# Two batches through both MLPs together, instead of batch 0 ahead: an attention and MoE kernel on one core

## The chip, the cores and the metric

The kernel runs on one core of one Trainium2 chip. The metric is the device time of one execution in microseconds. Three runs of the kernel before took 1252.75, 1256.22 and 1260.56 us; the median, 1256.22, is what a changed kernel is held against.

## The reference

Four batches of twelve heads, 448 tokens, head size 64, all inputs float32 (the weights arrive as float64 and are rounded). Attention's output, tokens by 768 features, goes through two bias-free MLPs in a row:

```python
q_n, k_n = rmsnorm(q, g_q), rmsnorm(k, g_k)
attn = softmax(q_n @ k_n.T / 8)                 # per head, with max subtracted and 1e-9 in the sum
x = (attn @ v), heads side by side              # (4 * 448, 768)
h = x @ w_in;  x = maximum(0.01 * h, h) @ w_out # 768 -> 2048 -> 768
a = x @ w1;  b = x @ w2                         # 768 -> 1024 each
out = ((a * b) @ w3) @ w_last                   # 1024 -> 1024 -> 768
```

## The kernel before

**Precision.** Every large product is made of three matmuls in float32r: a value is split into a high part (ScalarE copy) and a low part (subtraction on VectorE or GpSimd), and high x high, low x high, high x low are summed in PSUM (`group`, L519). Weights come as 64-bit words: `Weights.load` fetches a tile (a DMA to `w64`, two buffers), `to_float32` rebuilds float32 out of the words on GpSimd, ScalarE and VectorE, `split` makes `wh` and `wl`. `product` (L569) takes one weight tile and runs it over the batches that it is given; each batch's sum has a PSUM buffer of its own out of three.

**Attention** is a generator, `attention_steps`, of 50 slots of ten steps, one slot a head. A head is eight score matmuls (`ps`, L285 and L286), four readings of them on VectorE, four exponentials on ScalarE, sixteen transposes (`pt`), four copies of these; a pair of heads shares one group of sixteen value matmuls (`po`). The keys of a pair are prepared ahead: `kt` and `rk` are loaded into single buffers, scaled, split, and four DMAs spread the halves into `ks`, which has two buffers. The sum of the exponentials goes out to DRAM (`rd`) and comes back broadcast over partitions (`rb`). All DMAs are issued by SyncE, one after the other, and a DMA that has to wait holds back those behind it.

**Fillers.** `fill` walks through the attention's steps and puts in as many pieces of another generator as its planned nanoseconds allow. Before: slots 5 to 17 get `combine_weights` (w3 times w_last, tile `pw`); slots 17 to 25 get the first MLP's groups 0 and 1 for batch 0 alone (`early`); from slot 25 on come the same two groups for batch 1 (`late`), and then for both batches the first MLP's groups 2 and 3 and the second MLP's two groups. Since groups 0 and 1 are visited twice, their split parts are written to DRAM on the first visit (`kept_first_mlp_h`, `kept_first_mlp_l`, L488) and fetched back on the second (L472). The rounded float32 weights (`kept_first_mlp`, L477, and `kept_second_mlp`) are written in any case: after attention the last two batches run both MLPs from them, in seven products instead of eight (`last_pair`).

A scheduler with a simulated clock then fixes the order of each engine's instructions from this code order, priorities and dependences, so slots and the place of a filler need not agree.

Of the kernel before, what the change touches and what calls it, by code (L numbers as in the profile page):

```python
# [8 lines left out]
F32 = mybir.dt.float32  # L9
F32R = mybir.dt.float32r  # L10
# [7 lines left out]
B, H, S, D = 4, 12, 448, 64  # L18
NT = B * S
DM, FF, F2 = 768, 2048, 1024  # L20
P = 128
# [6 lines left out]
WT = DM  # L28
PB = 2
# [8 lines left out]
GROUPS = {0: 2, 2: 2, 4: 4, **{i: 8 for i in range(8, 48, 8)}}  # L38
MAX_GROUP = 8
TOGETHER = 2000  # L40
COMBINE_SLOTS = 5, 17
EARLY = 2
PRIORITY = dict(
    values=200, p_transpose=600, scores=600, prep=600, load=100, statistics=100, keys=50
)
# [3 lines left out]
def attention_then_moe(  # L49
# [22 lines left out]
    nc = tc.nc  # L72
# [324 lines left out]
    class Weights:  # L397
# [15 lines left out]

        def size(self, t):
            src, wide = self.sources[t][:2]
            if isinstance(src, tuple):
                return src[0].shape[1]
            return src.shape[1] // (2 if wide else 1)

        def load(self, t):  # L420
            src, wide = self.sources[t][:2]
            n = self.size(t)
            if isinstance(src, tuple):
                return
            if not wide:
                self.raw[t] = wp.tile([P, WT], F32, tag="raw", name="raw")
                nc.sync.dma_start(self.raw[t][:, :n], src)
                return
            x = self.words[t] = cv.tile([P, WT, 2], U32, tag="w64", name="w64")
            with tc.issue_after(start["ins"].ins) if t < 2 else ExitStack():  # L430
                nc.sync.dma_start(x[:, :n], src.rearrange("p (n t) -> p n t", t=2))
# [31 lines left out]
        def split(self, t):  # L463
            src, wide, keep, parts = self.sources[t]
            n = self.size(t)
            if isinstance(src, tuple):
                self.parts[t] = tuple(
                    wp.tile([P, WT // P, P], F32R, tag=tag, name=tag) for tag in ("wh", "wl")
                )
                for y, part in zip(self.parts[t], src):  # L470
                    y = y.rearrange("p k c -> p (k c)")[:, :n].bitcast(F32)
                    nc.sync.dma_start(y, part)  # L472
                self.ready = t + 1
                return
            x = self.raw.pop(t)[:, :n]
            if keep is not None:
                nc.sync.dma_start(keep[0], x)  # L477
            if parts is None:
                parts = tuple(
                    wp.tile([P, WT // P, P], F32R, tag=tag, name=tag) for tag in ("wh", "wl")  # L480
                )
                flat = [y.rearrange("p k c -> p (k c)")[:, :n] for y in parts]
            else:
                flat = parts
            nc.scalar.activation(flat[0], x, AF.Copy)  # L485
            subtract("V", flat[1], x, flat[0])
            for y, part in zip(flat, keep[1:] if keep else ()):
                nc.sync.dma_start(part, y.bitcast(F32))  # L488
            self.parts[t] = parts
            self.ready = t + 1  # L490

# [168 lines left out]

            yield from each(product(ws, bs, gs), result)

    kept, again = {}, {}

    def sources(plan):

        for f, bs, g in plan:
            if f is first_mlp:
                tiles = [w_in[g * KG + m] for m in range(KG)] + [w_out[g, m] for m in range(NO)]
            else:  # L670
                tiles = [w12[g * KH2 + m // 2, m % 2] for m in range(2 * KH2)]
            if (f, g) in kept:
                yield from ((k, False, None, None) for k in again[f, g])
            else:
                twice = sum(x[0] is f and x[2] == g for x in plan) > 1
                names = ("", "_h", "_l") if twice else ("",)
                ks = [
                    [
                        dram.tile([P, w.shape[1] // 2], F32, name=f"kept_{f.__name__}{g}_{i}{e}")
                        for e in names  # L680
                    ]
                    for i, w in enumerate(tiles)
                ]
                kept[f, g] = [k[0] for k in ks]
                again[f, g] = [tuple(k[1:]) for k in ks]
                yield from ((w, True, k, None) for w, k in zip(tiles, ks))
            if f is second_mlp:
                for m in range(NO):
                    w = wc[m, :, g * KH2 : (g + 1) * KH2].rearrange("p k c -> p (k c)")
                    yield w, False, None, None  # L690
# [292 lines left out]
    def plan_ns(plan):  # L983
        n = {first_mlp: KG * KD + NO * KG, second_mlp: 2 * KH2 * KD + NO * KH2}
        return sum(3 * S * NS * len(bs) * n[f] for f, bs, _ in plan)
# [25 lines left out]
    def fill(gen, total, span, until, begin=0):  # L1011

        spent, n = 0.0, 0
        done = False
        while True:
            at = next(steps, None)
            n += 1
            while not done and spent < total * (n - begin) / span:
                c = next(gen, None)
                if c is None:  # L1020
                    done = True
                else:
                    spent += c
            if at is None or at == until:
                break
        for _ in gen:
            pass

    parts_of = [(first_mlp, g) for g in range(NG)] + [(second_mlp, g) for g in range(2)]
    early = [(f, (0,), g) for f, g in parts_of[:EARLY]]  # L1030
    late = [(f, (1,), g) for f, g in parts_of[:EARLY]]
    late += [(f, (0, 1), g) for f, g in parts_of[EARLY:]]

    def run(pool, ws, plan):
        for f, bs, g in plan:
            yield from f(pool, ws, bs, g)

    with tc.tile_pool(name="comb", bufs=1) as pool:
        hi = pool.tile([P, K2, DM], F32R, name="lasth")
        lo = pool.tile([P, K2, DM], F32R, name="lastl")  # L1040
        ws = Weights(
            [
                w
                for k in range(K2)
                for h in range(2)
                for w in [
                    (w_last[j], True, None, (hi[:, j], lo[:, j]))
                    for j in range(h * KH2, (h + 1) * KH2)
                    if k == 0
                ]  # L1050
                + [(w3t[k, h], True, None, None)]
            ]
            + list(sources(early + late))
        )
        blocks = Blocks(list(last_sources()))
        n = slots[1] - slots[0]
        fill(combine_weights(ws, hi, lo), comb_ns, n * per_slot, slots[1], slots[0] * per_slot)
    pool = first_pair.enter_context(tc.tile_pool(name="mlp", bufs=1))
    n = PB * H + 1
    fill(run(pool, ws, early), plan_ns(early), (n - slots[1]) * per_slot, n)  # L1060
    fill(run(pool, ws, late), plan_ns(late), (B - PB) * H * per_slot, None)
    first_pair.close()
    last["pool"] = ctx.enter_context(tc.tile_pool(name="mlp2", bufs=1, reuse_waits="tile"))
    for _ in last_pair():
# [45 lines left out]
```

## Time and profile before

| | |
|---|---|
| median of three runs | 1256.22 us (1252.75 to 1260.56) |
| profiled execution | 1252.88 us, its span 1251.1 us |
| TensorE matmuls | 1151.0 us busy, 5816 |
| VectorE | 769.4 us busy |
| ScalarE | 661.4 us busy |
| GpSimd | 226.5 us busy |
| DMA | 191.44 MB, queue of SyncE 51.0% of 16 engines |
| mean granted clock of TensorE | 0.962 |

Matmuls overlap in their pipeline and their ends are modelled, so TensorE's busy time contains more than the time between two starts. The granted clock is 1.0 at 2.4 GHz and 0.5 at 1.2 GHz.

### The profile page before, as it was taken

To read this page: it belongs to the slowest core of one execution; us is meant where nothing else is said; L and a number is where in the kernel's file an instruction comes from. 1 tells how busy PE (TensorE), PEld (TensorE's weight loads), DVE (VectorE), ACT (ScalarE), POOL (GpSimd) and SP (SyncE) were. 2 spreads that over 40 slices of the span, in tenths; PEclk is the share of its full clock that TensorE was granted. 3 is DMA by queue.
4 is the path that set the end of the run, shared out by engine and by line. 5 is a ranking of instruction groups with operands and counts; after the bars stand their busy time and mean duration, and the time that the engine had idled before them with its cause. 6 is when DMAs were issued, how large, how long until landed. Compare 5 with 4: busy or idle time off the path is not lost.

```text
span 1251.1 us, 16792 instructions
## 1 busy us (share of the span) xinstructions
PE 1151.0 (92%) x5816; PEld 976.7 (78%) x5816; DVE 769.4 (61%) x1449; ACT 661.4 (53%) x1308; POOL 226.5 (18%) x211
## 2 busy tenths in 40 slices
PE   3659898999888999898999999999999999899998
PEld 1438686876566888686888888899999999799997
DVE  6788776779755466663785355267346465954553
ACT  5766766677656556454765465245442434533431
POOL 4232222334212123213542211100000000000000
PEclk9769999888998999998999999999999999899999
DMA  7777768989889975564464243153212121212212
GB/s 226 195 203 214 215 189 269 292 284 290 251 245 273 240 202 162 151 187 137 148 218 130 79 133 134 53 167 110 81 34 76 35 76 42 73 38 73 63 35 97
DMA packets 105221, 191.44 MB, mean 153 GB/s; under 512 B 22992, under 2 KB 61872, under 8 KB 105136
## 3 DMA queue, kind: packets, MB, share of 16 engines
q1 hardware_dynamic: 105136, 190.37, 51.0%
q8 instruction: 45, 0.74, 0.3%
q14 instruction: 40, 0.33, 0.1%
HBM read 136.74 MB, written 43.03 MB: 144 GB/s over the span
## 4 chain that ended last, share of the span: by engine, by line
PE 54%; DMA 14%; DVE 7%; ACT 4%; issue 3%; SPq 2%; POOL 1%; ACTq 0%; DVEq 0%; POOLq 0%
PE ps_mm L527 19%; PE ps_o L527 13%; PE ps_b L527 9%; PE ps_c L527 5%; DMA w<-w_in 3%; DMA w<-w_out 3%; PE ps_a L527 2%; PE pt L327 2%; PE po L121 2%; DMA ks<-kt_sb 2%; DMA kt_sb<-kt 1%; DMA wh<-kept_first_mlp_h 1%; PE ps L285 1%; DVE raw L460 1%; PE ps L286 1%
## 5 line engine op out<-in xcount | busy, mean ns | idle before, releaser
L213 DVE TENSOR_TENSOR wl<-raw,wh 128x512 fp32r<-128x512 f32 (+1 forms) x136 | 112.6, 831 | 73.0 <-ACT wh L485 37.8
L527 PE MATMUL ps_mm<-xh,wh 128*128 128x448 f32 x384 | 146.6, 383 | 10.6 <-DMA wh<-kept_first_mlp_h 6.9
L327 PE MATMUL pt<-ident,p 112*112 112x112 f32 x768 | 115.3, 276 | 42.2 <-ACT pth L101 21.3
L327 PEld LDWEIGHTS pt<-ident,p 112*112 112x112 f32 x768 | 88.1, 141 | 77.2 <-ACT pth L101 27.6
L289 DVE TENSOR_SCALAR_CACHE_REDUCE p<-ps,rs 112x448 f32<-112x448 f32 x192 | 126.1, 676 | 33.8 <-PE ps L286 20.4
L527 PE MATMUL ps_mm<-xh,wl 128*128 128x448 f32 x384 | 145.5, 379 | 1.5 <-DMA wl<-kept_first_mlp_l 1.5
L298 ACT ACTIVATE p<-p,low 112x448 f32<-112x448 f32 x192 | 127.2, 663 | 36.1 <-DVE p L289 35.7
L527 PE MATMUL ps_mm<-xl,wh 128*128 128x448 f32 x384 | 145.1, 378 | 0.0
L451 ACT ACTIVATE w<-w 128x768 uint32<-128x768 uint32 (+1 forms) x80 | 63.7, 797 | 109.3 <-DMA w<-w_in 36.2
L456 DVE SCALAR_TENSOR_TENSOR raw<-w,raw 128x768 uint32<-128x768 uint32 (+1 forms) x80 | 71.4, 892 | 79.9 <-ACT w L454 79.6
L449 POOL TENSOR_SCALAR raw<-w 128x768 f32<-128x768 f32 (+1 forms) x80 | 70.0, 875 | 265.8 <-DVE wl L213 99.5
L527 PE MATMUL ps_mm<-gh,wh 128*128 128x448 f32 x288 | 106.7, 372 | 2.7 <-DMA wh<-kept_first_mlp_h 1.3
L527 PE MATMUL ps_mm<-gh,wl 128*128 128x448 f32 x288 | 105.7, 369 | 0.0
L527 PE MATMUL ps_mm<-gl,wh 128*128 128x448 f32 x288 | 105.4, 367 | 0.0
L527 PE MATMUL ps_o<-gl,wh 128*128 128x448 f32 x288 | 104.7, 365 | 0.0
L527 PE MATMUL ps_o<-gh,wl 128*128 128x448 f32 x288 | 102.5, 365 | 0.0
L527 PE MATMUL ps_o<-gh,wh 128*128 128x448 f32 x288 | 99.4, 366 | 0.8 <-DVE s L940 0.8
L285 PE MATMUL ps<-ks,qh 128*112 128x448 f32 x192 | 80.2, 422 | 16.4 <-DMA ks<-kt_sb 6.7
L527 PEld LDWEIGHTS ps_mm<-xh,wh 128*128 128x128 f32 x384 | 75.1, 196 | 19.9 <-DMA wh<-kept_first_mlp_h 7.4
L213 POOL TENSOR_TENSOR gl<-y,gh 128x448 fp32r<-128x448 f32 x48 | 58.9, 1229 | 161.6 <-ACT gh L101 154.9
L527 PEld LDWEIGHTS ps_mm<-xh,wl 128*128 128x128 f32 x384 | 75.0, 195 | 10.5 <-issue 2.1
L213 POOL TENSOR_TENSOR ql<-qt_sb,qh 128x448 fp32r<-128x448 f32 x48 | 61.1, 1273 | 114.2 <-ACT qh L101 71.0
(129 smaller groups left out, 2556.1 us busy)
## 6 DMA issues: line engine op xcount, KB each, us to landing
w<-w_in SPq DMA_DIRECT2D x16, 768.0 KB, 7.4
w<-w_out SPq DMA_DIRECT2D x24, 512.0 KB, 5.2
w<-w SPq DMA_DIRECT2D x16, 768.0 KB, 4.9
qk_sb<-qk SPq DMA_DIRECT2D x48, 224.0 KB, 4.9
qt_sb<-qt SPq DMA_DIRECT2D x96, 112.0 KB, 4.0
w<-w3t SPq DMA_DIRECT2D x16, 512.0 KB, 4.6
w<-w_last SPq DMA_DIRECT2D x8, 768.0 KB, 6.2
kept_first_mlp<-raw SPq DMA_DIRECT2D x16, 384.0 KB, 4.0
```

Of the source, the lines that this page charges most:

```text
L121: one = nc.tensor.matmul(out, a, x, start=begin, stop=end)
L213: e.tensor_tensor(out, x, y.bitcast(F32), op=ALU.subtract)
L285: nc.tensor.matmul(ps, h["qh"][:, q], h["ks"], start=True, stop=False)
L286: nc.tensor.matmul(ps, h["ql"][:, q], h["ks"], start=False, stop=True)
L289: nc.vector.tensor_scalar(p, ps, h["scale"][:, c : c + 1], None, op0=ALU.mult, op1=ALU.min, accum_out=low,)
L298: exps[i] = nc.scalar.activation(p, p, AF.Exp, bias=low, scale=-1.0, accum_out=h["sum"][:, c : c + 1])
L327: nc.tensor.transpose(pt[:, c * CP : (c + 1) * CP], h["p"][c][:, kc * CP : (kc + 1) * CP], ident[:CP, :CP],)
L449: nc.gpsimd.tensor_scalar(out, h, 0.0, 1.0, op0=ALU.mult, op1=ALU.mult)
L451: nc.scalar.activation(low, low, AF.Copy, scale=2.0**-29)
L456: nc.vector.scalar_tensor_tensor(top, high, 3, top, op0=ALU.logical_shift_left, op1=ALU.bitwise_or)
L460: nc.vector.tensor_tensor(top, top, low, op=ALU.add)
L527: nc.tensor.matmul(ps[:, :n], a, x, start=begin, stop=end, skip_group_check=on)
```

## The change

Batches 0 and 1 go through all six groups together, from slot 25 on. There are no groups for batch 0 alone, hence no second visit and no parts of weights in DRAM: `Weights` loses the branches that wrote and fetched them. `combine_weights` is spread over slots 5 to 25. The number of matmuls on TensorE stays the same, 5620 rows of matmuls and transposes in the program; SyncE's program goes from 721 rows to 647 (a row can hold two like DMAs).

```diff
-COMBINE_SLOTS = 5, 17
-EARLY = 2
+COMBINE_SLOTS = 5, 25
...
         def split(self, t):
             src, wide, keep, parts = self.sources[t]
             n = self.size(t)
-            if isinstance(src, tuple):
-                self.parts[t] = tuple(
-                    wp.tile([P, WT // P, P], F32R, tag=tag, name=tag) for tag in ("wh", "wl")
-                )
-                for y, part in zip(self.parts[t], src):
-                    y = y.rearrange("p k c -> p (k c)")[:, :n].bitcast(F32)
-                    nc.sync.dma_start(y, part)
-                self.ready = t + 1
-                return
             x = self.raw.pop(t)[:, :n]
             if keep is not None:
-                nc.sync.dma_start(keep[0], x)
+                nc.sync.dma_start(keep, x)
...
             subtract("V", flat[1], x, flat[0])
-            for y, part in zip(flat, keep[1:] if keep else ()):
-                nc.sync.dma_start(part, y.bitcast(F32))
...
-    early = [(f, (0,), g) for f, g in parts_of[:EARLY]]
-    late = [(f, (1,), g) for f, g in parts_of[:EARLY]]
-    late += [(f, (0, 1), g) for f, g in parts_of[EARLY:]]
+    plan = [(f, (0, 1), g) for f, g in parts_of]
...
-    n = PB * H + 1
-    fill(run(pool, ws, early), plan_ns(early), (n - slots[1]) * per_slot, n)
-    fill(run(pool, ws, late), plan_ns(late), (B - PB) * H * per_slot, None)
+    fill(run(pool, ws, plan), plan_ns(plan), (B - PB) * H * per_slot, None)
```

The order of TensorE's instructions, before, in head 16 (of 0 to 47; `ps_mm` is a product of the first MLP, `gh` and `gl` the parts of batch 0's hidden layer):

```order
L527 MATMUL ps_mm_2980<-gl_2831,wh_2919 128x448
L527 MATMUL ps_mm_2980<-gh_2830,wl_2920 128x448
L527 MATMUL ps_mm_3029<-gh_2660,wh_2997 128x448
L527 MATMUL ps_mm_3029<-gl_2661,wh_2997 128x448
L527 MATMUL ps_mm_3029<-gh_2660,wl_2998 128x448
L527 MATMUL ps_mm_3029<-gh_2754,wh_2997 128x448
L527 MATMUL ps_mm_3029<-gl_2755,wh_2997 128x448
L327 MATMUL pt_2382<-ident_90,p_2287 112x112
L327 MATMUL pt_2382<-ident_90,p_2298 112x112
L327 MATMUL pt_2382<-ident_90,p_2317 112x112
L285 MATMUL ps_2457<-ks_1742,qh_2186 112x448
L286 MATMUL ps_2457<-ks_1742,ql_2188 112x448
```

And of the changed kernel, in head 18 (`xh_1897` and `xl_1898` are batch 1's features of the pair of heads just finished; the two `ps_mm` are sums of batch 1 that stay open until its last pair):

```order
L511 MATMUL ps_mm_3394<-xl_1898,wh_3224 128x448
L511 MATMUL ps_mm_3394<-xh_1897,wl_3225 128x448
L326 MATMUL pt_2293<-ident_90,p_2215 112x112
L326 MATMUL pt_2293<-ident_90,p_2222 112x112
L326 MATMUL pt_2293<-ident_90,p_2233 112x112
L284 MATMUL ps_2353<-ks_1761,qh_2140 112x448
L285 MATMUL ps_2353<-ks_1761,ql_2142 112x448
L326 MATMUL pt_2303<-ident_90,p_2215 112x112
L326 MATMUL pt_2303<-ident_90,p_2222 112x112
L326 MATMUL pt_2303<-ident_90,p_2233 112x112
```

Between the first score matmul of head 14 and that of head 26 there are 336 `ps_mm` matmuls before and 55 now; 13 more now stand in head 13. The 384 `pw` matmuls end in head 13 in both.

SyncE's order before, where the same stretch prepares a pair of heads:

```order
L268 DMA ks<-kh 64x448
L269 DMA ks<-kt_sb 64x448
L196 DMA qt_sb<-qt 64x448
L197 DMA qt_sb<-qt 64x448
L488 DMA kept_first_mlp_6_h<-wh 128x512
L488 DMA kept_first_mlp_6_l<-wl 128x512
L255 DMA kt_sb<-kt 128x448
L477 DMA kept_first_mlp_7_272<-raw 128x512
L431 DMA w_3145<-w_out 128x1024
L314 DMA rd_2334<-r 112x2x4
```

And now:

```order
L267 DMA ks<-kh 64x448
L268 DMA ks<-kt_sb 64x448
L195 DMA qt_sb<-qt 64x448
L196 DMA qt_sb<-qt 64x448
L254 DMA kt_sb<-kt 128x448
L145 DMA qk_sb<-qk 112x512
L313 DMA rd_2252<-r 112x2x4
L195 DMA qt_sb<-qt 64x448
L196 DMA qt_sb<-qt 64x448
L316 DMA rb<-rd_2252 64x448 x2
```

The weights' transfers between the attention's are gone: those of tile 6 and later now stand behind the last pair of batch 1, and the parts' nowhere.

## Rows read from the trace of the kernel before

**Rows 1.** Busy us (instructions) of engines by stretch, granted clock, DMA share, GB/s
```profile
core 0: us, PE busy (x) PEld busy (x) DVE busy (x) ACT busy (x) POOL busy (x), PEclk, DMA share, GB/s
210.40:370.00 159.60, 140.03 (x723) 109.16 (x722) 117.62 (x235) 110.29 (x239) 50.12 (x46) 0.93 0.90 277
370.00:442.10 72.10, 65.90 (x347) 53.24 (x346) 38.09 (x97) 43.13 (x101) 16.17 (x15) 0.94 0.96 253
442.10:614.80 172.70, 161.59 (x831) 135.61 (x830) 104.15 (x195) 91.19 (x187) 50.84 (x48) 0.98 0.53 160
614.80:856.40 241.60, 240.99 (x1256) 206.90 (x1254) 135.88 (x239) 120.54 (x227) 51.94 (x45) 1.00 0.43 138
856.40:1251.10 394.70, 386.29 (x1861) 349.77 (x1859) 214.97 (x352) 156.49 (x273) 0.00 (x0) 0.99 0.19 59
```
**Rows 2.** Chain of waits, 385 to 420 us: start us, us, what
```profile
388.62 0.20 PE ps L285
...
389.53 1.85 PE ps_mm L527 x9
...
392.58 3.16 PE po L121 x16
...
397.77 0.77 PE pt L327 x8
```
**Rows 3.** The same stretches, instructions on tile ps_mm alone
```profile
210.40:370.00 159.60, 82.61 (x336) 66.99 (x336) 3.55 (x6) 7.45 (x14) 0.93 0.90 277
370.00:442.10 72.10, 41.58 (x175) 33.37 (x174) 0.00 (x0) 7.48 (x14) 0.94 0.96 253
442.10:614.80 172.70, 127.51 (x577) 108.71 (x576) 13.92 (x23) 8.43 (x16) 0.98 0.53 160
614.80:856.40 241.60, 198.59 (x931) 172.94 (x930) 21.06 (x36) 14.82 (x28) 1.00 0.43 138
```
**Rows 4.** TensorE's waits, 341.5 to 442.1 us: us in total, times, longest
```profile
PE ps_mm L527 <- DMA wh<-kept_first_mlp_h: 7.2, 3, 5.6
```
**Rows 5.** DMA issues: count, KB each, median us from issue to landing
```profile
kept_first_mlp_h<-wh SPq DMA_DIRECT2D x12, 256.0 KB, 3.8
...
rd<-r SPq DMA_DIRECT2D x24, 3.5 KB, 4.2
```
**Rows 6.** Timeline of SyncE: start us, us, line, operation, count
```profile
324.20 1.10 SPq L269 DMA_DIRECT2D ks<-kt_sb  x2
```
**Rows 7.** Groups of instructions: count, busy us, mean ns, idle before, releasers
```profile
L289 DVE TENSOR_SCALAR_CACHE_REDUCE p<-ps,rs 112x448 f32<-112x448 f32 x192 | 126.1, 676 | 33.8 <-PE ps L286 20.4 <-PE pt L327 13.4
...
L103 DVE COPY pth<-pt 112x448 f32<-112x448 f32 x96 | 59.2, 617 | 36.4 <-PE pt L327 22.2 <-PE po L121 14.1
...
L150 DVE TENSOR_REDUCE ss<-qk_sb 112x8 f32<-112x512 f32 x48 | 32.5, 678 | 16.4 <-ACT qk_sb L149 16.1
...
L260 DVE SCALAR_TENSOR_TENSOR kt_sb<-kt_sb,gqk,rk_sb 128x448 f32<-128x448 f32 x23 | 17.4, 757 | 32.5 <-DMA kt_sb<-kt 14.4 <-DMA rk_sb<-rk 6.5 <-DMA rd<-r 5.5
...
L289 DVE DVE_READ_ACCUMULATOR p<-ps,rs 112x1 f32 x192 | 15.6, 81 | 0.0
```
**Rows 8.** Tile ks, 100 to 340 us: landing of its DMAs
```profile
DMA to landing us min/median/max: 2.2/4.3/6.7
```
**Rows 9.** SyncE's waits over the span: us in total, times, longest
```profile
SPq L317 <- DMA rd<-r: 39.4, 19, 5.4
...
SPq L314 <- DVE r L312: 31.2, 10, 5.8
SPq L255 <- DMA ks<-kt_sb: 30.7, 16, 4.0
```
**Rows 10.** Busy us by stretch around a fall of the clock, columns as in rows 1
```profile
361.90:368.70 6.80, 2.53 (x19) 1.80 (x18) 4.45 (x7) 6.29 (x12) 1.84 (x3) 1.00 0.59 141
368.70:372.10 3.40, 3.40 (x13) 2.92 (x12) 3.40 (x8) 1.24 (x4) 2.56 (x2) 0.50 0.84 228
```
**Rows 11.** Timeline of TensorE at half clock: start us, us
```profile
274.03 0.57 PE L527 MATMUL ps_mm<-xl,wh 128*128 128x448 f32 x1
274.41 0.57 PE L527 MATMUL ps_mm<-xh,wl 128*128 128x448 f32 x1
```

More of the change, by code (lines that the diff above doesn't have):

```diff
@@ L415, in size @@
             src, wide = self.sources[t][:2]
-            if isinstance(src, tuple):
-                return src[0].shape[1]
             return src.shape[1] // (2 if wide else 1)
@@ L422, in load @@
             n = self.size(t)
-            if isinstance(src, tuple):
-                return
             if not wide:
@@ L465, in split @@
             n = self.size(t)
-            if isinstance(src, tuple):
-                self.parts[t] = tuple(
-                    wp.tile([P, WT // P, P], F32R, tag=tag, name=tag) for tag in ("wh", "wl")
-                )
-                for y, part in zip(self.parts[t], src):
-                    y = y.rearrange("p k c -> p (k c)")[:, :n].bitcast(F32)
-                    nc.sync.dma_start(y, part)
-                self.ready = t + 1
-                return
             x = self.raw.pop(t)[:, :n]
             if keep is not None:
-                nc.sync.dma_start(keep[0], x)
+                nc.sync.dma_start(keep, x)
             if parts is None:
@@ L661, in second_mlp @@
             yield from each(product(ws, bs, gs), result)
-    kept, again = {}, {}
+    kept = {}
     def sources(plan):
@@ L671, in sources @@
                 tiles = [w12[g * KH2 + m // 2, m % 2] for m in range(2 * KH2)]
[L672 to L686, printed above, removed]
+            kept[f, g] = [
+                dram.tile([P, w.shape[1] // 2], F32, name=f"kept_{f.__name__}{g}_{i}")
+                for i, w in enumerate(tiles)
+            ]
+            yield from ((w, True, k, None) for w, k in zip(tiles, kept[f, g]))
             if f is second_mlp:
@@ L1052, in attention_then_moe @@
             ]
-            + list(sources(early + late))
+            + list(sources(plan))
         )
```

## The prediction

> **What bounds the kernel now.** I read the busy table by stretch first, cut at the first score matmul of certain heads (head h is the h-th group of eight score matmuls on TensorE). Seven stretches: A heads 0 to 4, B 5 to 13, C 14 to 25, D 26 to 31, E 32 to 39, F 40 to 47, G what follows the last product of batches 0 and 1 [rows 1]. TensorE is busy nearly all of F and G, and well short of it in C and D, where the DMA engines are busy 0.90 and 0.96 [rows 1]. So a busy share alone misleads; I turn it into a demand. The chain of waits gives undisturbed steps at the full clock: nine filler matmuls (128x448) in 1.85 us, so 0.206 us each; a score matmul 0.20; eight transposes 0.77; the sixteen value matmuls of a pair of heads 3.16 [rows 2]. A head asks TensorE for 8 x 0.20 + 2 x 0.77 + 3.16 / 2 = 4.7 us. The counts of filler (tile ps_mm) per stretch are 336, 174, 576, 930 for C to F; a matmul on a cut is shown on both sides [rows 3]. Demand against length:
>
> - C: 336 x 0.206 + 12 x 4.7 = 125.6 of 159.6 us, 34.0 lost
> - D: 174 x 0.206 + 6 x 4.7 = 64.0 of 72.1, 8.1 lost
> - E: 576 x 0.206 + 8 x 4.7 = 156.3 of 172.7, 16.4 lost, a ratio of 1.105
> - F: 930 x 0.206 + 8 x 4.7 = 229.2 of 241.6, 12.4 lost, a ratio of 1.054
>
> C and D lose 42 us between them. Part of it is the kept parts: in heads 24 to 31 TensorE waits 7.2 us for the first half of them alone [rows 4].
>
> **The change, part by part.** *Kept parts go.* Eight kinds of transfers fall away, 80 in all, of 256 or 384 KB, the smaller of which take 3.8 us and more to land [rows 5]: 4 x (8 x 384 + 12 x 256) KB, 25 MB, and at 0.55 us an issue [rows 6] 44 us of SyncE's time, nearly all in C and D. No arithmetic goes: batch 1's second visit split nothing, and now nothing is visited twice.
>
> *Fillers move.* TensorE does the same products. In A and B the order of after is nearly that of before (all 384 matmuls of w3 times w_last still stand ahead of head 14, though the slots now run to 25: the scheduler takes what is ready), so I let C begin at 210.4 as before [rows 1]. In C the order of after holds 55 fillers instead of 336: batch 1's x is not complete, two PSUM buffers hold its open sums, and nothing else may run. 13 more stand in B. So 2016 - 68 = 1948 fillers come after head 25, where before it was 1680. The 268 that move cost 268 x 0.206 = 55 us there. It has to be paid back by C becoming shorter: C and the rest are the two terms of the sum.
>
> *C without fillers: what is a head worth?* It asks TensorE for 4.7 + 55/12 x 0.206 = 5.6 us. VectorE: four score readings (126.1 + 15.6 us over 48 heads), two copies of transposes (59.2), statistics (32.5), the scaling of the keys (17.4): 250.8 / 48 = 5.2 us, and some small work [rows 7]. Neither is the bound. The loop of SyncE is: it issues in order, and for a pair of heads the order of after has 17 transfers (four ks, four qt, kt, two qk, rd, two rb, two rk, v), with nothing between them now that the weights are gone. 17 x 0.55 = 9.4 us. In that loop SyncE stands still twice: kt waits for ks to land, median 4.3 us of which two qt issues hide 1.1 [rows 8], and rb waits for rd to land, 4.2 us, of which one issue hides 0.6 [rows 5]. Sum 9.4 + 3.2 + 3.6 = 16.2 us, 8.1 a head. Lower end: with landings as short as the shortest ks, 2.2 us [rows 8], the pair is 9.4 + 1.1 + 1.6 = 12.1 us, 6.1 a head, close to TensorE's 5.6 and VectorE's 5.2 and more; no engine is kept full when three loops are that near, so I put the end at 7.0. Upper end: nothing gained, 159.6 / 12 = 13.3. I take 8.7: the loop of 8.1, and about 1.2 us a pair for what SyncE also waits for, the reciprocals and the split keys (r took 3.1 us each time it was late, rd 2.1, ks 1.9) [rows 9]. C becomes 12 x 8.7 = 104.4 us, and head 26 begins at 314.8 instead of 370.0.
>
> The Trainium skill's page "DMA: Bandwidth & Descriptors" (section "Latency and other measured facts") says that a lighter load on HBM makes the fixed part of a transfer smaller, which would push the loop to its lower end; with 12 x 7.0 us for C the sum below would be 20 us less. The landings of 2.2 to 6.7 us of one and the same transfer agree with a dependence on load.
>
> *After head 25.* The first MLP's other 1152 - 68 = 1084 fillers stand with heads 26 to 42 in the order of after: 1084 x 0.206 + 17 x 4.7 = 303.2 us. This is E's mixture (both batches, weights converted from 64 bits beside attention), so E's ratio: 335.0. The second MLP with five heads: 864 x 0.206 + 5 x 4.7 = 201.5, with F's ratio 212.4. 20 conversions move here too; they lie on VectorE, ScalarE and GpSimd, which were busy 0.60, 0.53 and 0.29 of E with the same density of them [rows 1], so they are paid by E's ratio and not again. If that cover is thin, D's ratio (72.1 / 64.0 = 1.127) adds 7 us; F's takes 15 off.
>
> *Sum.* 210.4 + 104.4 + 335.0 + 212.4 = 862.2 against 856.4: 5.8 us later. G is the same work, 394.7 us [rows 1]. The profiled execution took 1252.88 us (span 1251.1), so its counterpart is 1258.7; the median of the runs shown is 1256.22, 3.3 above that execution, so I state 1262.
>
> **Rivals.**
>
> *Attention runs free in C (faster).* If landings shorten as load falls, a head takes 7.0 us: 20.4 us less than my sum, 1241.6. For it: C's DMA share of 0.90 is mostly weights and kept parts. Against it: the waits of SyncE are round trips, and they stay. It decides below 7.6 us a head.
>
> *TensorE drops to half clock in C (slower).* From 368.7 to 372.1 us the granted clock was 0.50, which is the level of 1.2 GHz; just ahead of it TensorE had been busy 2.53 of 6.80 us [rows 10]. At that level fillers start 0.374 us apart [rows 11] instead of 0.206. C without fillers may look like that all along. If it ran at half clock, a head asks 4.7 x 0.374 / 0.206 + 4.6 x 0.374 = 10.3 us: TensorE becomes the bound, C is 123.6, and the time 1281. Against it: after 3.4 us, in which TensorE was busy without a gap, the clock came back [rows 10], so it should alternate. It decides from 9.4 us a head. The Trainium skill's page "TensorE: Matmul & The Clock Gate" (section "HAM oscillation — how this bites in real kernels") says that matmul bursts with waits between them fall back to the half rate again and again; it speaks against taking filler out of C.
>
> *The denser rest starves (slower).* After head 25 every product needs a freshly converted tile. If the ratio of the first MLP is 1.17, between E's and the 1.27 of C now (159.6 / 125.6), it costs 303.2 x 0.065 = 19.7 us more: 1282. C's 1.27 included the kept parts' transfers, which speaks against it.
>
> **How the numbers follow.** The forecast (a head in C between 7.6 and 9.4 us, ratio near E's) has 0.43; attention free 0.25; half clock 0.20; starved rest 0.12. A measurement of this kernel can tell about 1% (12.6 us) from no change. The forecast falls within it: same 0.43, faster 0.25, slower 0.32. The likeliest alone reaches from 7.6 to 9.4 us a head, 1249 to 1270. The range for 8 in 10 takes in part of both sides: the low end is 7.3 us a head with a ratio 1.08 (-16.8 and -7.6, 1238); the high end 10.3 us a head and D's ratio (+19.2 and +6.7, 1288).
>
> **What would show it.** Right: head 26 near 315 us, heads 14 to 25 at 8 to 9.4 us each, SyncE waiting on rd and ks landings there, TensorE's demand met within 10% from there to 862, G at 395. Wrong: head 26 before 302 or after 323; a granted clock near 0.5 through C; TensorE waiting for wh behind ScalarE after head 26; or A and B changing by more than 3 us.

## The result, and the profile after

The changed kernel took 1265.02 us (median of 13 runs, 1259.47 to 1270.42), the kernel before 1257.69 us in the same comparison (13 runs, 1248.83 to 1260.56). The ratio of the two, over runs compared with each other, is 1.0073, with a 95% interval of 1.0053 to 1.0092 (the medians alone give 1.0058): slower by 0.7%, within the 1% that the prediction set as its bound, and 3 us above its 1262. The profiled execution took 1264.04 us, span 1262.3 us.

Busy us by stretch of the changed kernel, columns as in [rows 1]; the stretches are B (heads 5 to 13), C (14 to 25), D (26 to 31), E (32 to 39), F (40 to 47) and G, cut at the first score matmul of the same heads as before, wherever those now begin:

```profile
core 0: us, PE busy (x) PEld busy (x) DVE busy (x) ACT busy (x) POOL busy (x), PEclk, DMA share, GB/s
90.70:219.20 128.50, 116.48 (x646) 98.25 (x647) 94.94 (x197) 84.27 (x184) 29.72 (x29) 0.94 0.72 204
219.20:322.60 103.40, 84.36 (x436) 54.38 (x435) 66.60 (x174) 66.90 (x165) 25.05 (x21) 0.90 0.60 147
322.60:402.00 79.40, 77.47 (x422) 64.58 (x421) 60.65 (x122) 58.91 (x128) 23.66 (x23) 1.00 0.68 199
402.00:569.50 167.50, 152.67 (x781) 124.66 (x780) 97.92 (x192) 90.12 (x184) 42.20 (x42) 0.98 0.51 154
569.50:867.40 297.90, 294.06 (x1503) 255.28 (x1502) 158.85 (x269) 144.72 (x270) 72.98 (x66) 0.99 0.42 137
867.40:1262.30 394.90, 386.01 (x1861) 349.65 (x1860) 214.61 (x352) 156.22 (x273) 0.00 (x0) 0.99 0.19 59
```

And the same stretches from C on, instructions on tile `ps_mm` alone, as in [rows 3]:

```profile
219.20:322.60 103.40, 15.79 (x56) 10.88 (x55) 0.00 (x0) 0.53 (x1) 0.90 0.60 147
322.60:402.00 79.40, 54.83 (x247) 45.72 (x247) 0.00 (x0) 9.97 (x19) 1.00 0.68 199
402.00:569.50 167.50, 114.07 (x520) 97.22 (x519) 12.91 (x21) 8.44 (x16) 0.98 0.51 154
569.50:867.40 297.90, 251.51 (x1183) 221.83 (x1182) 25.96 (x42) 19.12 (x36) 0.99 0.42 137
```

C is 56 us shorter than in [rows 1] and holds 55 fillers instead of 336. D, E and F together are 544.8 us instead of 486.4, 58.4 us longer, and hold what C lost. The DMA share of C went from 0.90 to 0.60 and that of D from 0.96 to 0.68, and TensorE no longer waits for a kept part [rows 4]. So both halves of the change did what they say, and the time hardly moved.

The prediction's method makes this a balance: demand is 0.206 us a filler plus 4.7 us a head, and what a stretch takes beyond it is lost. The third column is the first experiment below, the last two belong to the order of the instructions.

| us | before | after | resplit | sens_act | ord_sc |
|---|---|---|---|---|---|
| heads 0 to 13 (A, B) | 210.4 | 219.2 | 214.1 | 218.4 | 216.8 |
| lost in C | 34.0 | 35.7 | 26.5 | 29.5 | 42.7 |
| lost in D | 8.1 | 0.3 | 1.9 | 0.2 | 3.6 |
| lost in E | 16.4 | 23.0 | 10.5 | 15.4 | 19.1 |
| lost in F | 12.4 | 16.8 | 13.2 | 14.8 | 20.0 |
| lost in C to F | 70.9 | 75.8 | 52.1 | 59.9 | 85.4 |
| demand of C to F | 575.1 | 572.4 | 575.1 | 571.8 | 572.0 |
| G | 394.7 | 394.9 | 395.6 | 395.8 | 394.8 |
| span | 1251.1 | 1262.3 | 1236.9 | 1245.8 | 1269.0 |

After against before: 8.8 us in A and B, 4.9 us more lost in C to F, 2.7 us less demand there (13 fillers moved into head 13), 0.2 us in G; in sum the 11.2 us between the spans. C loses as much as before, although only 67.7 of its 125.6 us of TensorE demand are left.

**What a bare head waits for.** From head 16 on the even heads of C are short (4.6 to 5.9 us), the odd ones long (10.1 to 13.3 us); the sixteen value matmuls of a pair stand in the odd one. TensorE's waits in C, in us in total, times, longest:

```profile
PE ps L284 <- DVE p L288: 11.4, 13, 4.6
PE pt L326 <- DVE pth L102: 6.2, 5, 2.6
PE ps_mm L511 <- POOL xl L212: 0.7, 1, 0.7
PE pt L326 <- ACT pth L100: 0.6, 2, 0.3
```

A score matmul waits because both `ps` buffers are full and VectorE hasn't read them, a transpose because VectorE hasn't emptied `pt`. VectorE is busy 66.6 of C's 103.4 us, so it isn't short of time. Head 25 shows what it does instead, in the chain of waits (start us, us, what):

```profile
309.41 3.72 DMA kt_sb<-kt
...
313.15 0.04 DVE kt_sb L259
...
313.75 0.63 DVE pth L102
...
314.43 0.85 PE pt L326 x6
315.28 4.76 PE po L120 x16
```

VectorE stands at `kt_sb` (L259, the scaling of a later pair's keys) until that pair's keys have landed at 313.13; the copy `pth`, which needs nothing from a DMA, stands behind it in VectorE's order. TensorE's timeline, with the idle time and its releaser in brackets, and the stretches around it, columns as above:

```profile
314.43 0.85 PE L326 MATMUL pt<-ident,p 112*112 112x112 f32 x6 [2.60 <-DVE pth L102]
```
```profile
311.60:315.00 3.40, 0.80 (x9) 0.58 (x7) 1.85 (x5) 1.12 (x2) 0.41 (x1) 1.00 0.40 86
315.00:318.40 3.40, 3.40 (x13) 1.16 (x12) 1.80 (x4) 1.93 (x5) 0.00 (x0) 0.50 0.54 158
```

TensorE waited 2.60 us, was busy 0.80 of 3.40 us, and the granted clock fell to 0.50, the level of 1.2 GHz. The sixteen value matmuls then took 4.76 us instead of 3.16 [rows 2], and `x` (L363), the scaling of their result, stood 3.05 us on VectorE waiting for them. Head 21 has the longest of these stands, in VectorE's timeline and then TensorE's:

```profile
285.17 0.69 DVE L259 SCALAR_TENSOR_TENSOR kt_sb<-kt_sb,gqk,rk_sb 128x448 f32<-128x448 f32 x1 [5.69 <-DMA rk_sb<-rk]
285.77 0.68 DVE L288 TENSOR_SCALAR_CACHE_REDUCE p<-ps,rs 112x448 f32<-112x448 f32 x1
```
```profile
286.51 0.71 PE L284 MATMUL ps<-ks,qh 128*112 128x448 f32 x1 [4.62 <-DVE p L288]
```

Here VectorE waits 5.69 us for the keys' scale on its way back from DRAM (`rk_sb`), the reading `p` of scores long finished stands behind, and TensorE waits 4.62 us for its buffer. In that wait, at 284.3 us, the granted clock falls to 0.50 for 6.8 us:

```profile
284.30:291.10 6.80, 4.58 (x18) 3.92 (x19) 5.33 (x13) 4.46 (x12) 2.68 (x2) 0.50 0.65 172
```

VectorE's longer waits in C, in us in total, times, longest:

```profile
DVE x L363 <- PE po L120: 8.1, 3, 3.4
DVE kt_sb L259 <- DMA rk_sb<-rk: 5.7, 1, 5.7
...
DVE kt_sb L259 <- DMA kt_sb<-kt: 3.4, 2, 2.3
DVE x L363 <- DMA rb<-rd: 3.0, 1, 3.0
```

Of the 35.7 us lost in C, the four waits of TensorE shown above are 18.9 us, and 20.5 us at the half level cost at most half of that, 10.2 us. The rest, 6.6 us or more, is not accounted for.

SyncE's own waits in C are small beside what the prediction put there, 12 us at `rb` and `kt` in sum for six pairs:

```profile
SPq L316 <- DMA rd<-r: 9.3, 5, 2.6
SPq L267 <- PE ps L285: 9.2, 5, 2.9
...
SPq L254 <- DMA ks<-kt_sb: 2.4, 5, 1.1
```

The landings of `ks` had become shorter. For heads 14 to 25, first before and then after:

```profile
DMA to landing us min/median/max: 2.3/5.0/9.6
DMA to landing us min/median/max: 2.1/2.3/3.0
```

### The profile page after: what moved, and what is told of

Its sections match the earlier page's. It is cut to its first block, busy times and chain, and to the rows that moved or that the text cites. A ratio compares the mean times of both kernels' runs of the same rounds, so it can differ in the third digit from the quotient of the medians.

```text
span 1262.3 us, 16659 instructions
## 1 busy us (share of the span) xinstructions
PE 1158.1 (92%) x5816; PEld 975.6 (77%) x5816; DVE 763.7 (61%) x1449; ACT 658.7 (52%) x1308; POOL 222.4 (18%) x211
## 4 chain that ended last, share of the span: by engine, by line
PE 56%; DMA 21%; DVE 12%; ACT 5%; SPq 3%; issue 3%; POOL 1%; DVEq 0%; ACTq 0%; POOLq 0%
PE ps_mm L511 19%; PE ps_o L511 12%; PE ps_b L511 9%; PE ps_c L511 5%; DMA ks<-kt_sb 4%; DMA w<-w_in 4%; PE po L120 3%; DMA w<-w 2%; PE ps_a L511 2%; PE pt L326 2%; DVE raw L451 2%; DMA w<-w_out 2%; DVE raw L455 2%; DMA kt_sb<-kt 2%; DMA rk<-rs 2%
## 5 line engine op out<-in xcount | busy, mean ns | idle before, releaser
L326 PE MATMUL pt<-ident,p 112*112 112x112 f32 x768 | 118.2, 279 | 46.5 <-ACT pth L100 23.0
L511 PE MATMUL ps_mm<-xl,wh 128*128 128x448 f32 x384 | 142.0, 370 | 0.7 <-POOL xl L212 0.7
L511 PE MATMUL ps_mm<-xh,wh 128*128 128x448 f32 x384 | 141.9, 372 | 0.0
L511 PE MATMUL ps_mm<-xh,wl 128*128 128x448 f32 x384 | 141.5, 368 | 0.0
L288 DVE TENSOR_SCALAR_CACHE_REDUCE p<-ps,rs 112x448 f32<-112x448 f32 x192 | 126.0, 677 | 11.4 <-PE ps L285 6.7
L284 PE MATMUL ps<-ks,qh 128*112 128x448 f32 x192 | 83.4, 439 | 29.3 <-DVE p L288 15.5
L120 PE MATMUL po<-pth,v_sb 112*64 112x448 f32 x384 | 87.3, 601 | 0.0
L449 ACT ACTIVATE w<-w 128x768 f32<-128x768 f32 (+1 forms) x80 | 62.9, 786 | 35.8 <-POOL raw L444 35.7
L511 PEld LDWEIGHTS ps_mm<-xh,wh 128*128 128x128 f32 x384 | 72.2, 189 | 10.5 <-issue 2.1
```

Of the source, the lines that this page charges most:

```text
L120: one = nc.tensor.matmul(out, a, x, start=begin, stop=end)
L284: nc.tensor.matmul(ps, h["qh"][:, q], h["ks"], start=True, stop=False)
L288: nc.vector.tensor_scalar(p, ps, h["scale"][:, c : c + 1], None, op0=ALU.mult, op1=ALU.min, accum_out=low,)
L326: nc.tensor.transpose(pt[:, c * CP : (c + 1) * CP], h["p"][c][:, kc * CP : (kc + 1) * CP], ident[:CP, :CP],)
L449: nc.scalar.activation(h, h, AF.Copy, scale=2.0**-112)
L511: nc.tensor.matmul(ps[:, :n], a, x, start=begin, stop=end, skip_group_check=on)
```

## The experiments

All but early1 were built from the changed kernel (resplit3 by way of resplit), and the diffs are against that; the stretches are named as above. Each ratio is to the kernel before, run beside it; that kernel's median differs from one comparison to the next (1246.09 to 1257.69 us), so ratios are compared across them, and times only where the text says so. "Head" is one head's length, from its first score matmul to that of the next.

### The two halves apart

**resplit**: fillers for batch 0 alone in slots 17 to 25 as before, but batch 1's visit loads the kept float32 weights and splits them again. Nothing is written or fetched as parts.

```diff
-COMBINE_SLOTS = 5, 25
+COMBINE_SLOTS = 5, 17
+EARLY = 2
...
+            if (f, g) in kept:
+                yield from ((k, False, None, None) for k in kept[f, g])
+                continue
...
-    plan = [(f, (0, 1), g) for f, g in parts_of]
+    early = [(f, (0,), g) for f, g in parts_of[:EARLY]]
+    late = [(f, (1,), g) for f, g in parts_of[:EARLY]]
+    late += [(f, (0, 1), g) for f, g in parts_of[EARLY:]]
...
```

> The kernel before, but the second visit of groups 0 and 1 (batch 1) loads the rounded float32 weights that are kept anyway and splits them again; the split parts are neither written nor read (40 writes and 20 reads fewer, 20 splits more). Theory (the parts' transport is what makes heads 14 to 31 lose 42 us against TensorE's demand): heads 14 to 25 fall from 159.6 us to 138 to 148, heads 26 to 31 stay near 72, the whole 1235 to 1247. Rival (TensorE, VectorE and ScalarE set that stretch, the transport hides behind them): 159 us as before, the whole 1254 to 1260. Second rival (the 20 splits cost more than the reads they replace): heads 26 to 31 longer than 80 us, the whole above 1260.

Measured: 1239.45 us against 1249.68 before, ratio 0.9917 (0.9884 to 0.9951). It is faster than both kernels. The whole and D (72.1 us) came as the theory had them; C, at 152.1 us, lies above its 138 to 148. Busy by stretch, C to F:

```profile
214.10:366.20 152.10, 137.26 (x721) 105.23 (x718) 115.28 (x234) 107.43 (x232) 46.83 (x42) 0.97 0.70 207
366.20:438.30 72.10, 71.47 (x400) 58.20 (x399) 52.28 (x115) 51.94 (x119) 18.81 (x16) 1.00 0.59 158
438.30:598.90 160.60, 153.56 (x783) 130.68 (x782) 105.01 (x198) 95.58 (x191) 50.03 (x48) 0.97 0.58 180
598.90:841.30 242.40, 241.02 (x1255) 207.22 (x1254) 135.54 (x237) 119.73 (x226) 51.55 (x45) 1.00 0.42 136
```

C still has its 336 fillers and loses 26.5 us instead of 34.0; D, at the same length as before, holds 204 fillers instead of 174; E loses 10.5 instead of 16.4. In sum C to F lose 52.1 us instead of 70.9, 18.8 us less; A and B are 3.7 us longer, and the span is 14.2 us shorter. So the kept parts did cost more than splitting the twenty tiles a second time; the order of the engines moved too, so the 18.8 us are no clean price. It is the change without its other half, and it gains 0.8%; against it the changed kernel, at 1.0073, is 1.6% slower (1.0073 / 0.9917 = 1.016). Without batch 0's early fillers C to F lose 23.7 us more, 9.2 of them in C and 12.5 in E. That is where the gain went, as far as these two orders show it (what an order alone can move is measured further down).

**early1**: the kernel before with one group for batch 0 alone instead of two.

```diff
-EARLY = 2
+EARLY = 1
```

> The kernel before with EARLY = 1: one group of the first MLP for batch 0 alone instead of two, so half of the parts are written and fetched back, and heads 14 to 25 hold 191 fillers instead of 336 (before) or 55 (after). Theory (two halves that add: the kept parts cost about 10 us of the median, the missing fillers of heads 14 to 25 about 25, both in proportion): half of each, -5 + 13 = about +8 us, a ratio to before of 1.002 to 1.011. Rival (the kept parts cost only because C and D are full of transfers, so that half of them is nearly free): -10 + 13 = +3 us or less, 0.996 to 1.002.

Measured: 1249.76 us against 1252.08 before, ratio 1.0002 (0.9976 to 1.0028). That is the rival's range, below the theory's: the two halves don't scale as the theory had it. Heads 20 to 25, with 30 fillers in all, last 8.8 us each, as bare as after's. Why half of the parts costs so little isn't shown by it.

**resplit3**: resplit with a third group for batch 0 alone.

```diff
-EARLY = 2
+EARLY = 3
```

> The kernel that splits the kept float32 weights again on batch 1's visit, with EARLY = 3: a third group of the first MLP for batch 0 alone, so that heads 23 to 25, which held 12 fillers in that kernel and lasted 24.3 us for 12 x 0.206 + 3 x 4.7 = 16.6 us of TensorE's demand, hold 92. Theory (each bare head loses what TensorE can't use, 2.6 us, and a filler there brings it back): 4 to 8 us below the kernel with two groups, a ratio to before of 0.985 to 0.990. Rival (a third group split twice costs VectorE, ScalarE and GpSimd more than the three heads give, since 8 more tiles are fetched and split a second time): 0.990 or above.

Measured: 1242.77 us against 1252.08 before, ratio 0.9924 (0.9899 to 0.995). The rival's range: no better than two groups. Heads 23 to 25 went from 24.3 to 40.6 us for 80 fillers more, 16.5 us of demand, so the time grew by the full price of the fillers, and the bare heads' loss wasn't won back.

### Where the combining of w3 and w_last stands

**slots17**: the changed kernel with the old slots for `combine_weights`, and the MLPs still from slot 25 on.

```diff
-COMBINE_SLOTS = 5, 25
+COMBINE_SLOTS = 5, 17
...
+    for at in steps:
+        if at == PB * H + 1:
+            break
```

> The changed kernel with w3 times w_last planned over slots 5 to 17 as before, and no filler planned from slot 17 to 25. Theory (the scheduler takes fillers as soon as they are ready, so the slots' numbers hardly matter): within 4 us of the changed kernel, 1261 to 1269, and heads 5 to 13 at 121 to 130 us. Rival (the spread over slots 5 to 25 is what made heads 5 to 13 8 us longer): heads 5 to 13 back at 121 us and the whole 1255 to 1259.

Measured: 1265.11 us against 1249.68, ratio 1.0112 (1.0077 to 1.0147). B is 119.9 us, as the rival had it and about as before, but the whole is not faster: C is 111.9 us instead of 103.4, and the sum of B and C 231.8 us, in after 231.9.

**spread7**: the slots kept at 5 to 25, and the loads of the combining's later weights held back behind a load of queries some slots earlier, so that its products reach to head 16 instead of 13.

```diff
-        dma = nc.sync.dma_start(h["qt"][D:P], qt[b, j])
+        dma = start[i] = nc.sync.dma_start(h["qt"][D:P], qt[b, j])
+        start["latest"] = start.get(i - 7)
...
-            with tc.issue_after(start["ins"].ins) if t < 2 else ExitStack():
+            behind = start["ins"] if t < 2 else start["latest"] if K2 < t < 3 * K2 else None
+            with tc.issue_after(behind.ins) if behind else ExitStack():
```

> The changed kernel, with each load of a w3 tile queued on SyncE behind a load of q that attention makes some slots earlier: the 384 matmuls of w3 times w_last now stand in heads 3 to 16 instead of 3 to 13, about 30 and then 24 a head. Theory (a head without filler takes 8.6 us whatever TensorE has to spare, and TensorE has some 3 us to spare in it): heads 5 to 25 fall from 232 us to 212 to 222, the whole 1247 to 1257. Rival (what leaves heads 8 to 13 costs the same in heads 14 to 16): 232 us, the whole 1262 to 1268.

Measured: 1262.03 us, ratio 1.0093 (1.0063 to 1.0123). B is 115.4, C 117.3, in sum 232.7 us: the rival's numbers. Within these intervals the new slots of the diff are worth nothing either way, and the 8.8 us that A and B grew are not lost by them: B and C come to 232 us in after, slots17 and spread7, however the 384 products lie in them. That is no fixed sum; in the other orders below it is 221.2 (sens_act), 224.9 (xpool) and 234.3 (ord_sc).

### What sets a bare head

Four kernels add work to one engine each and nothing to the others; each ran once. In after, heads 16 to 25 last 8.32 us each, heads 20 to 25 8.77.

**sens_sp**: four more small transfers a head on SyncE.

```diff
+        for e in range(4):
+            spare = dram.tile([D, 16], F32, name=f"spare{i}_{e}")
+            nc.sync.dma_start(spare, qt[b, j][:, e * 16 : (e + 1) * 16])
```

> The changed kernel with four more small DMAs a head (64 pieces of 64 B from q into DRAM, never read, waiting for nothing), issued by SyncE behind each head's loads of q. Heads without filler (the last six or so before batch 1 is complete) take 8.3 us each in the changed kernel. Theory (SyncE's issues and waits set a bare head): 4 x 0.55 = 2.2 us more a head, 10.0 to 10.8. Rival (SyncE has slack, a head is set by what TensorE, VectorE and ScalarE hand to each other): 8.2 to 8.9.

**sens_dve**: the statistics' reduction three times instead of once.

```diff
+        for _ in range(3):
-        nc.vector.tensor_reduce(
+            nc.vector.tensor_reduce(
```

> The changed kernel with the sum of squares on VectorE (0.68 us a head) done three times over, same result. Heads without filler take 8.3 us in the changed kernel. Theory (SyncE sets a bare head): 8.2 to 8.8. Rival (VectorE sets it): 1.36 us more a head, 9.4 to 9.9.

**sens_pe**: the high x high score matmul three times instead of once; each restarts the sum, so eight more matmuls a head.

```diff
-        nc.tensor.matmul(ps, h["qh"][:, q], h["ks"], start=True, stop=False)
+        for e in range(3):
+            nc.tensor.matmul(ps, h["qh"][:, q], h["ks"], start=True, stop=e < 2)
```

> The changed kernel with each first score matmul done three times over (two results are written over): eight more matmuls of 0.20 us a head. Heads without filler take 8.3 us in the changed kernel. Theory (SyncE sets a bare head, TensorE has time to spare): 8.3 to 9.0, and after head 25, where TensorE is full, 1.6 us more a head, some 35 us. Rival (TensorE at half clock sets it): the extra work keeps the clock up, so as short as before or shorter, below 8.3, and less time at half clock in heads 14 to 25 than the 20 us of the changed kernel. Second rival (TensorE is on the path of a bare head in any case): 9.6 to 10.

**sens_act**, run later: the high part of the queries copied three times on ScalarE.

```diff
-        copy("A", h["qh"], h["qt"])
+        for _ in range(3):
+            copy("A", h["qh"], h["qt"])
```

> The changed kernel, with the high part of a head's queries copied three times on ScalarE instead of once: two more copies of 0.57 us a head (the trace of after has 13 of them, 566 ns each, in heads 14 to 25), 1.13 us of ScalarE a head and nothing else. Its order leaves heads 16 to 25 with 48 fillers in all, so they are compared with heads 16 to 25 of after, 8.33 us a head (heads 20 to 25: 8.76). Theory (a bare head is as long as the hand-over from TensorE's scores through VectorE's reading and ScalarE's exponentials to the transposes, and no engine's sum of work sets it; the copies of the queries are made ahead of that chain): 8.0 to 9.0 us a head. Rival (ScalarE's in-order queue sets a bare head, its exponentials standing behind the copies): 9.3 to 9.9 us.

Measured, heads 20 to 25 of after, sens_sp, sens_dve, sens_act and sens_pe, one row of the busy table each. They hold 18 fillers (sens_sp 20), so they can be compared; heads 16 to 25 hold 31 fillers in after, but 48 to 68 in the last three.

```profile
270.00:322.60 52.60, 40.64 (x206) 25.82 (x207) 33.25 (x88) 31.01 (x78) 10.22 (x9) 0.87 0.58 137
308.30:356.50 48.20, 37.96 (x210) 24.86 (x208) 31.60 (x81) 32.23 (x81) 11.54 (x11) 0.96 0.62 154
288.50:335.90 47.40, 39.57 (x212) 25.49 (x211) 41.42 (x106) 31.73 (x79) 10.04 (x9) 0.93 0.57 150
266.20:314.60 48.40, 38.37 (x217) 24.50 (x215) 34.15 (x90) 36.77 (x91) 10.52 (x9) 0.96 0.55 144
278.20:333.40 55.20, 47.14 (x259) 32.53 (x259) 34.68 (x88) 31.76 (x79) 10.34 (x9) 0.97 0.51 130
```

| | added a head | a head in 20 to 25 | whole kernel, one run (before beside it) |
|---|---|---|---|
| after | | 8.77 | 1264.04 (1257.69) |
| sens_sp | 4 issues on SyncE | 8.03 | 1301.77 (1249.84) |
| sens_dve | 1.36 us of VectorE | 7.90 | 1282.99 (1249.84) |
| sens_act | 1.13 us of ScalarE | 8.07 | 1247.67 (1252.08) |
| sens_pe | 1.6 us of TensorE | 9.20 | 1293.53 (1249.84) |

sens_sp and sens_dve came out just below the ranges that leave their engine room, sens_act inside its own. Neither SyncE's issues nor VectorE's or ScalarE's busy time sets a bare head; all three have room. So the prediction's loop on SyncE falls as the reason. Of TensorE's 1.6 us, 0.43 came, between the theory's range and the second rival's. The order of the engines moves in each of the four, and the orders without added work (slots17, spread7, ord_sc) have 8.36 to 8.59 us here, so a difference of some tenths a head means nothing: whether TensorE's own work is on the path of a bare head isn't shown. After head 25, where the theory had some 35 us more, sens_pe took 563.8 instead of 544.8 us. Where SyncE's issues did cost is among the fillers: sens_sp's span is 37.7 us longer, and its combining of weights, done in head 13 in after, still has 193 products to go at head 14.

**xpool**: `x` (L363), the scaling that waits for the value matmuls and for the reciprocals' way through DRAM, leaves VectorE: ScalarE copies `po`, GpSimd scales it.

```diff
-        nc.vector.tensor_tensor(x, po[:, :S], pair[1]["rb"], op=ALU.mult)
+        copy("A", x, po[:, :S])
+        nc.gpsimd.tensor_tensor(x, x, pair[1]["rb"], op=ALU.mult)
```

> The changed kernel, with x = po times rb taken off VectorE: ScalarE copies po out of PSUM and GpSimd multiplies with rb. VectorE then waits neither for the value matmuls nor for rb. Theory as in the prediction (SyncE's waits for the landings of rd and ks set a bare head's 8.6 us): heads 14 to 25 stay at 100 to 106 us, the whole 1260 to 1270. Rival (x stands on VectorE ahead of the next score readings and holds them back until the values and rb are there): heads 14 to 25 fall to 85 to 93 us, the whole 1248 to 1256. Second rival (ScalarE takes over the same waiting): 103 us or more.

Measured: 1259.15 us against 1249.68, ratio 1.0073 (1.0051 to 1.0095), the same ratio as after's. TensorE's waits in its C (214.0 to 312.4):

```profile
PE pt L326 <- DVE pth L102: 6.1, 8, 3.1
PE ps L284 <- DVE p L288: 2.0, 4, 1.2
```

No range holds for C: 98.4 us lies between the theory's and the rival's. But C also holds 66 fillers and 17 products of w3 and w_last here, in after 55 fillers. Its heads 20 to 25, with 18 fillers as in after, show the bare heads:

```profile
270.90:312.40 41.50, 37.52 (x208) 24.92 (x207) 31.07 (x83) 31.74 (x80) 11.30 (x10) 0.94 0.53 137
```

That is 6.92 us a head instead of 8.77, with the same transfers on SyncE, and 1.0 us below the shortest of the kernels with `x` on VectorE whose heads 20 to 25 are given above (7.90 to 9.20 us). VectorE's waits at `x` (8.1 and 3.0 us in after's C) are gone, and TensorE's wait for VectorE's readings of the scores goes from 11.4 to 2.0 us; the wait for `pth` stays, 6.1 us in C. So VectorE's stand at `x` is a cause of long bare heads, as far as one kernel against these shows it. How much of the 1.85 us it is by itself isn't known, since the order moved and the granted clock rose from 0.87 to 0.94. VectorE's stand at `kt_sb` is read from the trace of after, and wasn't taken away by itself.

In the ratio of the whole none of this shows. The span, 1255.0 us, is 7.3 us shorter than after's, but the kernel before ran 8.0 us faster beside it. E is 176.3 us instead of 167.5, with 606 fillers instead of 519, and loses 13.9 us instead of 23.0; D loses 9.2 instead of 0.3.

**resplit_xpool**: the same edit in resplit (both diffs above).

> Two parts at once, on the kernel before: groups 0 and 1 split again from the kept float32 weights (no parts in DRAM), and x made by ScalarE and GpSimd instead of VectorE. Theory (the first part is worth 10 us; the second shortens nothing where TensorE has filler): as the first part alone, 1234 to 1246 beside a kernel before of 1250. Rival (VectorE, busy 0.85 in heads 14 to 25, gains by it): 1225 to 1234.

Measured: 1252.59 us against 1249.84, ratio 1.0019 (1.0002 to 1.0036), about 1% slower than resplit by the two ratios, and in neither range. Its C is 149.9 us (resplit 152.1), its B 128.9 (121.0), its E 176.8 (160.6) with 556 fillers (546). Where fillers stand between the heads, taking `x` off VectorE won little and B and E became longer; whether by the copies on ScalarE or by the order isn't shown.

### What the order is worth

sens_act surprised: with more work than after it took 1247.67 us, 0.9965 of the 1252.08 of the kernel before beside it. The fastest of after's 13 runs is at 1.0014 of its own kernel before (1259.47 against 1257.69). The heads 14 to 25 of sens_act last 96.2 us and its heads 26 to 47 535.4 (after: 103.4 and 544.8). The extra copies had changed the scheduler's order.

**ord_sc**: the changed kernel with one number of the scheduler's priorities raised, so that the same instructions stand in another order, near that of sens_act.

```diff
-    values=200, p_transpose=600, scores=600, prep=600, load=100, statistics=100, keys=50
+    values=200, p_transpose=600, scores=650, prep=600, load=100, statistics=100, keys=50
```

> The changed kernel, every instruction the same, with the scheduler's priority of the score matmuls raised from 600 to 650: the order of the engines differs. It is near that of the kernel with two more copies on ScalarE, which in one look took 1247.67 us and had heads 14 to 25 in 96.2 and heads 26 to 47 in 535.5 us, for all that it had more work (of after: 103.4 and 544.8): in both, heads 16 to 25 hold 48 fillers, and heads 36, 40, 42, 44 and 46 hold 152, 192, 104, 128 and 94 (159, 192, 103, 123, 92 there). Theory (the order in which the fillers and the attention's steps stand is worth about 1% by itself, as much as the whole change): a ratio to before of 0.993 to 1.002, heads 14 to 25 in 93 to 100 us and heads 26 to 47 in 532 to 540. Rival (the one look was low by chance, or the two copies themselves help; the order does nothing): 1.004 to 1.012.

Measured: 1271.63 us against 1246.09, ratio 1.0198 (1.0153 to 1.0243). Neither range holds: it is slower than after, by 1.2% by the two ratios, with every instruction the same. The waits of TensorE in C, first ord_sc (216.8 to 326.8), then sens_act (218.4 to 314.6):

```profile
PE ps L284 <- DVE p L288: 11.5, 10, 5.1
PE pt L326 <- DVE pth L102: 6.4, 7, 2.7
PE ps_mm L511 <- ACT xh L100: 5.1, 2, 4.9
```
```profile
PE pt L327 <- DVE pth L102: 11.6, 10, 3.0
PE ps L285 <- DVE p L289: 4.1, 6, 2.2
```

In ord_sc the waits of over 4 us are back, in sens_act the longest is 3.0. So the order alone moves this kernel by about 1%, as much as the change does. Which step VectorE stands at when a transfer is late differs with it: its longest wait for a DMA in C is 4.2 us in ord_sc, at `x` for `rb`, and 5.7 us in after, at `kt_sb` for `rk_sb`. It isn't known what of sens_act's order helped.

## Why the prediction was right, and where it was not

- **The sum held.** 862.2 us was forecast for the end of F, 867.4 came; 5.8 us over before was forecast, 11.0 came. The time was 1265.02 against 1262 in a range of 1238 to 1288, and it falls where 0.43 of the chance lay, within 1%. The forecast's own ratio to before, 1.0046, lies just below the interval measured, 1.0053 to 1.0092.
- **A and B were the term that failed.** They were carried over unchanged to 210.4; C began at 219.2. The step took the order of instructions being nearly the same for the time being the same. Head 26 began at 322.6 instead of 314.8: these 8.8 us, less the 1.0 us by which C was shorter than forecast. The prediction had listed more than 3 us here as wrong. Slots17 and spread7 show that it isn't a cost of the new slots: there B and C trade it. What else made A and B longer isn't shown.
- **C, by its size right, and by luck.** Forecast 8.7 us a head, 104.4 in all; measured 103.4, 8.62 a head. The same instructions in another order took 110.0 us (ord_sc), and sens_act, with more of them, 96.2.
- **C, by its reason wrong.** The number came from SyncE's loop: seventeen issues and two waits for landings. Four more issues a head didn't lengthen a bare head, and SyncE's waits at those two places were 11.7 us in six pairs instead of the (3.2 + 3.6) x 6 = 41. With the landings that came, 2.3 us for `ks` and 3.2 for `rd`, the loop's own sum is 9.4 + 1.2 + 2.6 = 13.2 us a pair, 6.6 a head. The transfers are in the path, but VectorE waits for them (and for the value matmuls), with readings of scores and copies of transposes behind it in its queue, and TensorE behind those. The step that failed named the engine that issues the transfer, and not the one that stands in order behind its landing.
- **First rival, attention free (7.0 us a head).** Its condition came, its time did not: C's DMA share fell from 0.90 to 0.60 and the median landing of `ks` from 5.0 to 2.3 us, but a head took 8.62. Only xpool, which takes `x` off VectorE, has heads of 6.92 us. The prediction set the landing of `ks` beside the Trainium skill's page "DMA: Bandwidth & Descriptors" (section "Latency and other measured facts"), by which a lighter load on HBM shortens the fixed part; the broadcasts `rb` out of DRAM agree with the page, from a median of 4.4 to 3.1 us in C. `ks`, though, goes from one on-chip tile to another, so the page doesn't cover it.
- **Second rival, TensorE at half clock (10.3 us a head).** In C 20.5 of 103.4 us were at the level of 1.2 GHz, in pieces of 3.4 to 6.8 us: it alternated, as the forecast said. The two falls shown above, of five in C, came in or right behind a wait of TensorE of 2.6 us or more, so there the half clock lengthened a wait rather than making it. The Trainium skill's page "TensorE: Matmul & The Clock Gate" (section "HAM oscillation — how this bites in real kernels") describes just this back and forth; the price here was at most 10.2 us of C.
- **Third rival, the rest starves (ratio 1.17).** D to F came to 544.8 us against 547.4 forecast, and by the demand of 504.7 used there a ratio of 1.079. Heads 26 to 42 hold 1014 fillers in the trace instead of the 1084 counted, and took 315.5 us, a ratio of 1.092 where E's 1.105 was used. E by itself, at 167.5 / 144.5 = 1.16, did starve more, though it holds 519 fillers instead of 576: its loss grew from 16.4 to 23.0 us, and TensorE's waits for ScalarE's copies `pth` from 5.5 to 9.2 us there. D, freed of the kept parts, made up for it: 0.3 us lost instead of 8.1.
- **Kept parts.** They were taken out of the sum by giving D and E one ratio; resplit shows what they were worth by themselves, 0.8%. That this gain and the loss of the early fillers nearly cancel was in the sum, but was nowhere said in it as two numbers.
- **What stays open.** How much of the 0.7% belongs to the plan and how much to the order that the scheduler happened to find. Five kernels without early fillers (after, slots17, spread7, xpool, ord_sc) have ratios of 1.007 to 1.020; sens_act, in one run, was below 1. With early fillers and without parts, resplit and resplit3 are at 0.992 and resplit_xpool at 1.002. The two groups lie apart (xpool and resplit_xpool, which differ by the early fillers and the twenty splits, by 0.5%), but the order alone moves one of them by more than that.

## What to carry to other kernels

Take a change that both removes transfers and removes the work that filled an attention's gaps apart before judging it: here the first half alone was worth 0.8%, and the second, by the difference of two ratios, gave more than that back. In a stretch without filler, look for the in-order engine that stands at a value that a DMA or another engine still owes it, while steps that are ready queue behind; the engine with most busy time need not be it, nor the one that issues the transfer. And where a scheduler makes the order, build the same kernel in a second order before a change of 1% is put down to the plan.

## What the runs showed of the hardware

- SyncE had room in the bare heads: with four more issues a head they lasted 8.03 us (8.77 without), while among weights' loads the same issues came with a span 37.7 us longer.
- A wait of 2.60 us on TensorE, with 0.80 of 3.40 us busy, was followed by 3.40 us at a granted clock of 0.50; the sixteen value matmuls that began in it took 4.76 us, at the full clock 3.16 [rows 2].
- With the score matmuls tripled in part, the granted clock of heads 20 to 25 was 0.97 instead of 0.87, and a head was 0.43 us longer, with 1.6 us more work of TensorE in it.
- When `x`, which waits for the value matmuls and for a value on its way through DRAM, left VectorE, heads 20 to 25 lasted 6.92 us each instead of 8.77, with the same transfers.
- With C's DMA share at 0.60 instead of 0.90, the same on-chip transfers `ks` landed in a median of 2.3 us instead of 5.0.
- Splitting weights again from the float32 copy (172.57 MB moved in all) was faster than fetching the parts back (191.44 MB): 0.9917.
